# A two-attention kernel whose instruction order is planned by a built-in clock: rounded-part copies issued ahead, transfers modelled in order of arrival

## The chip, the cores and the metric

The kernel runs on one core of one Trainium2 chip. The metric is the device time of one execution in microseconds (us), lower is better. Three runs of the kernel before gave 1972.74, 1975.59 and 1976.52 us; the median is 1975.59 us.

## What is computed

Two attention layers read inputs of their own (x of 2048 x 1024, a joint weight wqkv of 1024 x 3072, an output weight wo of 1024 x 1024, all float32) and their outputs are put side by side. Both have 32 heads of width 32. Layer B is a sliding window of 256 keys. Layer A is a dilated window: 8 keys at distances 0, 2, ..., 14.

```python
def _B_ref(x, wqkv, wo):
    qkv = (x @ wqkv) split into q, k, v of 32 heads x 32
    scores = einsum("bhqd,bhkd->bhqk", q, k) * 32 ** -0.5
    scores = where(0 <= query - key < 256, scores, -1e9)
    return concat_heads(einsum("bhqk,bhkd->bhqd", softmax(scores), v)) @ wo

def _A_ref(x, wqkv, wo):
    # the same with keys at query - 0, 2, 4, ..., 14 (8 of them)
    ...

return concatenate([_A_ref(A_x, ...), _B_ref(B_x, ...)], axis=-1)
```

## The kernel before, in words

**Units and steps.** The 2048 positions of each layer are cut in 4 units of 512 (layer A is first sorted into even and odd positions, so that its window becomes 8 neighbouring keys). Units 0 to 3 are layer B ("dense", a band of 384 keys per 128 queries), units 4 to 7 are layer A ("window", a band of 136). A unit has 8 steps, one for each group of 4 heads: 64 steps in all, numbered hg = 8 * unit + s. All large products are made in three terms: each float32 operand is split into a part rounded to a short format (index 0) and the remainder (index 1), and the product is high x high + high x low + low x high (`TERMS`).

**What a step does.** (1) `qk_items` (L298) multiplies the unit's x by a Q weight and then a K weight: 24 matmuls each, L363. (2) `evac` (L311) brings a result out of PSUM: ScalarE (ACT) writes the rounded part (L314), VectorE (DVE) the remainder (L318) of the tile `nat`. (3) `stack` (L323) has the SyncE queue (SP) issue three SBUF to SBUF copies (L328) that put rounded part and remainder below one another in `qst` (order rounded, rounded, remainder) or `kst` (rounded, remainder, rounded). For units that look back across their border it also reads the last unit's keys (`read_halo`, L304), and writes its own for the next unit. There are two buffers `qst` and two `kst`, used by turns, so the copies of step hg must wait until step hg-2 has read its own. (4) The first pass (`first`, L599): 16 matmuls of scores (L614, called "one" below), each followed by a DVE maximum (L619) and an ACT exponential with a sum (L624). (5) The sums of a step go through a logarithm (L637), a small transpose on PE (`rows`, L653), a copy on DVE (L657) and an SP copy into rows 96 and 97 of `qst` (L660): these are the "row values", the softmax's offset, so that (6) the second pass (L696 dense, L509 window, called "two") gives normalised probabilities straight from an exponential. (7) Masks, then `values` (L741, L548) multiplies by V; `finish` (L570) splits the result for the output product (L577, L581).

**Other streams.** `v_items` makes V in four parts of a unit (L415), `o_items` (L438) multiplies the finished unit by wo (L455), copies the result out of PSUM (`copy_out`, L377: ACT or DVE, whichever the clock believes free earlier) into the one output buffer (`NST = 1`) and stores it from the ACT queue. `Stream` (L87) loads raw weights and x into 3 buffers from the GpSimd queue (POOL), and `parts` (L126) splits each: a cast on DVE, then the subtraction on DVE or POOL.

**What sets the order.** Nothing is scheduled by the compiler. A `Clock` (L33) keeps a believed time for each engine. The main loop (L803) asks the four sequences aux (`rows`), second pass, first pass, gemm (qk, v and o in the order of `plan`) when their next item could start, and puts the earliest on PE; follow-up work is put on its engine when the believed time has come. So a believed duration moves instructions in the program, and on the chip each engine runs its own list strictly in that order, waiting where a semaphore isn't there yet. Believed times of transfers come from `copy`, `load`, `fetch` and `move` (L53 to L76): two believed queues, "copies" (SP) and "loads" (ACT and POOL), that slow each other when both are busy; a copy is believed to start only when the remainder is done. A first pass may be put as soon as `done["stack"]` is believed reached, a second pass when `h["rows"]` is (L661).

**The banks.** Seven PSUM banks are used in rings: 3 for gemm results (`rg`), 4 for scores (`rs`), plus one for the attention output (`ro`).

**The end.** The last unit's output product has no other work to hide behind. The first `TAIL` = 2 output blocks run their first 7 of 8 parts before the last step is finished, and the rest follows (L789 to L797).

Of the kernel before, what the change touches and what calls it, by code (L numbers as in the profile page):

```python
# [25 lines left out]
O_SLOTS = {2: (0, 1), 3: (2, 3), 4: (4, 5), 5: (6, 7)}  # L26
NX, NST = 10, 1
TAIL, LAND, XAT = 2, 0.45, 1
# [4 lines left out]
class Clock:  # L33
# [5 lines left out]
    def __init__(self):  # L39
        self.free = dict(pe=0.0, act=0.0, dve=0.0, pool=0.0, sp=0.0, copies=0.0, loads=0.0)  # L40
        self.later, self.lands = [], []
        self.n = 0
# [9 lines left out]

    def copy(self, dur, *ready):  # L53

        return self.move("copies", "loads", self.use("sp", 0.63, *ready, self.lane()) + 0.4, dur)

    def load(self, dur, *ready):

        return self.move("loads", "copies", self.use("act", 0.35, *ready, self.lane()) + 0.45, dur)

    def fetch(self, dur, *ready):

        t = max(self.use("pool", 1.0, *ready) + 0.6, self.free["loads"])
        self.free["loads"] = t + dur + 0.5 * max(0.0, min(2 * dur, self.free["copies"] - t))
        return self.free["loads"] + LAND
# [21 lines left out]
class Stream:  # L87
# [10 lines left out]
    def load_to(self, n):  # L98
        while self.loaded < min(n, len(self.items)):
# [4 lines left out]
            self.raw[self.loaded] = raw, (self.ck.load if early else self.ck.fetch)(1.9, self.ck.now)  # L104
            self.loaded += 1

    def split_to(self, n):
        while self.split < min(n, len(self.items)):
# [3 lines left out]
            if self.items[i][0] == "x":  # L112
# [10 lines left out]
            end = self.ready[i] if self.items[i][0] != "x" else max(self.ready[i])  # L123
# [23 lines left out]
def kernel(ctx, tc, xs, wqk, wv, wo, outs, units):  # L147
# [23 lines left out]
    for u in range(U):  # L171
        for s in range(NG):
# [3 lines left out]
            if s in V_SLOTS:  # L176
                plan.append(("v", u, V_SLOTS[s]))
# [17 lines left out]
    for p in plan:  # L195
        ly = units[p[1]][0]
        if p[0] == "o":
            item(p, "w", wo[ly, p[2]])
# [99 lines left out]
    def qk_items(u, s):  # L298
# [5 lines left out]
        def read_halo():  # L304
            w = 256 if dense else 128
            hb = halo[(u + 1) % 2][s]
            for r, a in enumerate((0, 1, 0)):
                nc.sync.dma_start(kst[buf][r:96:3, :, 256 - w:256].bitcast(F32), hb[:, a, 256 - w:])
                ck.copy(0.55 if dense else 0.35, ck.now)

        def evac(t, ps, bank):  # L311
# [5 lines left out]
            def low():  # L317
# [556 lines left out]
```

## Time and profile before

| what | value |
|---|---|
| median of 3 runs | 1975.59 us (1972.74 to 1976.52) |
| the profiled execution's own time | 1973.82 us |
| its span, first to last instruction | 1972.1 us |
| granted TensorE clock, mean | 0.987 |
| PE busy | 1924.7 us (98%), 12608 matmuls |
| DVE, ACT, POOL busy | 66%, 49%, 36% |
| DMA, mean over the span | 150 GB/s; SP's queue 26.1% of the engines' time, POOL's loads 22.9% |
| first matmul | at 8.05 us |
| last matmul group (L455) | 1933.17 to 1968.5 us |

The page's chain of work that ended last lies on PE for 84% of the span, on DVE 7%, on DMA 6% and on ACT 2%. A busy PE in this profile includes matmuls that overlap: a matmul of 512 columns shows 401 ns, but the next one starts 227 ns after it when nothing is in the way. So in this text the cost of PE work is the distance from start to start, taken from the trace: 227 ns for 512 columns, 119 ns for 256, 177 ns for a first or second pass of 384, about 85 to 112 ns for one of 136 or 128. Where that distance is longer, PE waited, or ran at half its clock (427 ns).

### The profile page before, as it was taken

To read this page: it belongs to the slowest core of one execution; us is meant where nothing else is said; L and a number is where in the kernel's file an instruction comes from. 1 tells how busy PE (TensorE), PEld (TensorE's weight loads), DVE (VectorE), ACT (ScalarE), POOL (GpSimd) and SP (SyncE) were. 2 spreads that over 40 slices of the span, in tenths; PEclk is the share of its full clock that TensorE was granted. 3 is DMA by queue.
4 is the path that set the end of the run, shared out by engine and by line. 5 is a ranking of instruction groups with operands and counts; after the bars stand their busy time and mean duration, and the time that the engine had idled before them with its cause. 6 is when DMAs were issued, how large, how long until landed. Compare 5 with 4: busy or idle time off the path is not lost.

```text
span 1972.1 us, 36479 instructions
## 1 busy us (share of the span) xinstructions
PE 1924.7 (98%) x12608; PEld 1619.8 (82%) x12608; DVE 1295.7 (66%) x3762; ACT 957.5 (49%) x3137; POOL 708.7 (36%) x923
## 2 busy tenths in 40 slices
PE   7999999999999999999999999999999999999998
PEld 6878887888877878788878888978888788888886
DVE  5687776678665786567865657655666557666653
ACT  3565554475654656555563344423534334434441
POOL 4334343444433434443443323233332333233221
PEclk9999999999999999999999999999989999999998
DMA  5555546455546465345645647455553565556442
GB/s 176 150 139 153 160 124 178 132 153 157 152 136 174 121 189 149 117 140 148 177 119 146 173 139 196 128 149 170 149 163 116 174 177 162 141 146 172 136 126 75
DMA packets 136502, 294.92 MB, mean 150 GB/s; under 512 B 14464, under 2 KB 42112, under 8 KB 136320
## 3 DMA queue, kind: packets, MB, share of 16 engines
q1 hardware_dynamic: 85632, 124.82, 26.1%
q0 software_dynamic: 40320, 146.82, 22.9%
q10 hardware_dynamic: 10368, 20.98, 2.9%
q8 instruction: 100, 1.64, 0.4%
q14 instruction: 82, 0.67, 0.1%
HBM read 163.58 MB, written 27.26 MB: 97 GB/s over the span
## 4 chain that ended last, share of the span: by engine, by line
PE 84%; DVE 7%; DMA 6%; ACT 2%; issue 1%; SPq 0%; POOL 0%; DVEq 0%; ACTq 0%; POOLq 0%
PE g L363 31%; PE g L455 16%; PE g L415 16%; PE s L614 7%; PE s L696 5%; PE o L741 4%; PE s L509 3%; DMA qst<-rt 3%; PE o L548 2%; DMA kst<-nat 1%; DMA raw<-xs 1%; DVE x L137 1%; DVE w L129 1%; ACT s L624 1%; DVE w L137 1%
## 5 line engine op out<-in xcount | busy, mean ns | idle before, releaser
L363 PE MATMUL g<-x,w 128*128 128x512 f32 x3072 | 801.9, 401 | 8.6 <-DVE w L129 8.0
L134 POOL TENSOR_TENSOR w<-raw,w 128x512 fp32r<-128x512 f32 x225 | 392.5, 1745 | 897.2 <-PE s L614 285.7
L363 PEld LDWEIGHTS g<-x,w 128*128 128x128 f32 x3072 | 562.0, 191 | 110.9 <-DVE w L129 8.4
L624 ACT ACTIVATE s<-s,nm 128x384 f32<-128x384 f32 (+3 forms) x1024 | 452.3, 443 | 231.0 <-DVE nm L619 227.1
L415 PE MATMUL g<-w,x 128*128 128x256 f32 x3072 | 413.3, 285 | 0.0
L415 PEld LDWEIGHTS g<-w,x 128*128 128x128 f32 x3072 | 392.7, 191 | 1.9 <-issue 0.6
L455 PE MATMUL g<-ot,w 128*128 128x512 f32 x1536 | 384.2, 397 | 3.6 <-DVE w L129 2.9
L455 PEld LDWEIGHTS g<-ot,w 128*128 128x128 f32 x1536 | 283.8, 190 | 58.1 <-DVE w L129 3.6
L619 DVE CUSTOM_DVE_ANT_0 s<-s,mask_d 128x384 f32<-128x384 f32 (+2 forms) x512 | 262.0, 556 | 72.9 <-PE s L614 71.5
L614 PE MATMUL s<-kst,qst 96*128 96x384 f32 (+3 forms) x1024 | 238.7, 303 | 16.2 <-ACT s L624 7.1
L701 ACT ACTIVATE pbuf<-s 128x384 f32<-128x384 f32 (+2 forms) x480 | 197.1, 507 | 85.5 <-PE s L696 81.8
L614 PEld LDWEIGHTS s<-kst,qst 96*128 96x128 f32 x1024 | 181.3, 192 | 60.5 <-ACT s L624 18.1
L624 ACT ACTIVATION_READ_ACCUMULATOR s<-s,nm 128x1 f32 x1024 | 210.2, 205 | 0.0
L619 DVE CUSTOM_DVE_ANT_0 s<-s,mask_w 128x136 f32<-128x136 f32 (+1 forms) x512 | 142.4, 322 | 98.4 <-PE s L614 96.8
L129 DVE CAST w<-raw 128x1024 fp32r<-128x1024 f32 x256 | 199.9, 781 | 9.4 <-PE g L455 9.4
L137 DVE TENSOR_TENSOR w<-raw,w 128x512 fp32r<-128x512 f32 x287 | 197.2, 696 | 8.8
L682 POOL TENSOR_SCALAR_AFFINE_SELECT pbuf<-pbuf 128x128 f32<-128x128 f32 (+1 forms) x383 | 147.9, 404 | 150.1 <-ACT pbuf L701 143.5
L314 ACT ACTIVATE nat<-g 128x512 fp32r<-128x512 f32 x128 | 76.6, 598 | 255.2 <-PE g L363 247.8
L318 DVE SCALAR_TENSOR_TENSOR nat<-g,nat 128x512 fp32r<-128x512 f32 x128 | 88.3, 690 | 145.5 <-ACT nat L314 134.9
L524 DVE TENSOR_TENSOR pbuf<-pbuf,keep_w 128x272 f32<-128x272 f32 (+1 forms) x224 | 116.9, 566 | 61.5 <-ACT pbuf L514 60.6
L619 DVE DVE_READ_ACCUMULATOR2_ANT nm<- 128x1 f32 x1024 | 144.3, 141 | 0.0
L696 PEld LDWEIGHTS s<-qst,kst 98*128 98x128 f32 x704 | 106.2, 189 | 37.8 <-PE o L741 10.0
(48 smaller groups left out, 1227.3 us busy)
## 6 DMA issues: line engine op xcount, KB each, us to landing
raw<-wqk POOLq DMA_DIRECT2D x126, 512.0 KB, 3.7
qst<-nat SPq DMA_DIRECT2D x192, 256.0 KB
kst<-nat SPq DMA_DIRECT2D x192, 256.0 KB
raw<-wo POOLq DMA_DIRECT2D x64, 512.0 KB, 3.7
raw<-wv POOLq DMA_DIRECT2D x62, 512.0 KB, 4.5
outs<-ost ACTq DMA_DIRECT2D x64, 256.0 KB
raw<-xs POOLq DMA_DIRECT2D x28, 512.0 KB, 4.8
halo<-nat SPq DMA_DIRECT2D x40, 256.0 KB
```

The lines of the kernel that those rows point to most:

```text
L129: nc.vector.tensor_copy(t[:, 0, :], raw)
L134: nc.gpsimd.tensor_tensor(o, a, b, op=ALU.subtract)
L137: nc.vector.tensor_tensor(o, a, b, op=ALU.subtract)
L363: nc.tensor.matmul(h["ps"], h["w"][:, a, k * P:(k + 1) * P], xt[u][k][:, b, :], start=(k == 0 and i == 0), stop=(k == NK - 1 and i == 2))
L415: nc.tensor.matmul(ps, xt[u][k][:, a, p0:p0 + P], h["w"][:, c, k % kw], start=(k == 0 and i == 0 and r == 0), stop=(k == NK - 1 and i == 2 ...
L455: nc.tensor.matmul(h["ps"], h["w"][:, a, k * P:(k + 1) * P], ot[u, k][:, b, :], start=(k == 0 and i == 0), stop=(k == NK - 1 and i == 2))
L614: nc.tensor.matmul(ps[:, :n], q[0:96, j, b * P:(b + 1) * P], kk[0:96, j, c0:c1], start=True, stop=True)
L619: nc.vector.tensor_tensor_reduce(ps[:, :n], ps[:, :n], mask[:, cut:full], scale=-1.0, scalar=BIG, op0=ALU.add, op1=ALU.min, accum_out=nm)
L624: nc.scalar.activation(ps[:, :n], ps[:, :n], AF.Exp, bias=nm, scale=-1.0, accum_out=sm)
L682: nc.gpsimd.affine_select(w, w, pattern=[[0, m], [step, n]], compare_op=ALU.is_ge, fill=0.0, base=base, channel_multiplier=chan)
L696: nc.tensor.matmul(ps[:, i * n:(i + 1) * n], kk[0:98, j, 256 + kb * P:256 + (kb + 1) * P], q[0:98, j, q0:q0 + n], start=True, stop=True)
L701: nc.scalar.activation(w, ps[:, :pack * n].rearrange("p (j n) -> p j n", j=pack), AF.Exp)
```

## The change

It is one change to the planner and to what it plans with; no product, mask or sum is changed.

- *The transfers' model.* The two believed queues become one: every transfer takes its place in the order of arrival (`issue`, `move`), with new lead times, and a raw load of 1.95 us can stand ahead of a copy.
- *Rounded parts ahead.* `stack` is cut in two: `stack_hi` issues the copies of the rounded part when ACT has made it, and `stack` the copy of the remainder when DVE has made that. `read_halo` moves from the K to the Q copies. For K the order becomes rounded, rounded, remainder.
- *Later row values.* `LATE` = 0.4 us is added to the believed landing of the row values, and 30 columns to the believed DVE maximum. The believed landing of the keys, `done["stack"]`, gets no such addition in the diff.
- *V of the first unit* is placed after steps 0, 2, 4, 7 (before: 0, 1, 5, 7).
- *The end.* `TAIL` = 4, the fourth output block takes its bank from the score ring, and the weights of the last five blocks are split as two half tiles each from x's pool ("xw"), so that three weight tiles aren't the limit.

```diff
+V0_SLOTS = {0:0,2:1,4:2,7:3}
...
-TAIL, LAND, XAT = 2, 0.45, 1
+LATE = 0.4
+TAIL, LAND, XAT = 4, 0.45, 1
...
+    def issue(self, eng, hold, lead, dur, *ready):
+        start = max((self.free[eng],) + ready)
+        self.free[eng] = start + hold
+        return self.move(start + lead, dur)
...
     def copy(self, dur, *ready):
-        return self.move("copies", "loads", self.use("sp", 0.63, *ready, self.lane()) + 0.4, dur)
+        self.lands.append(self.issue("sp", 0.63, 1.25, dur, *ready, self.lane()))
+        return self.lands[-1]
...
-    def move(self, q, other, t, dur):
-        t = max(t, self.free[q])
-        self.free[q] = t + dur + 0.5 * max(0.0, min(2 * dur, self.free[other] - t))
-        self.lands.append(self.free[q] + LAND)
-        return self.lands[-1]
+    def move(self, t, dur):
+        busy = self.busy = [x for x in self.busy if x[1] > self.now - 20.0]
+        i = 0
+        while i < len(busy):
+            if busy[i][1] <= t or busy[i][0] < t:
+                t = max(t, busy[i][1])
+            elif busy[i][0] - t >= dur:
+                break
+            else:
+                t = busy[i][1]
+            i += 1
+        busy.insert(i, (t, t + dur))
+        return t + dur + LAND
...
                 def stack():
-                    if t == 1 and has_halo:
-                        read_halo()
-                    dst, c = (qst[buf], 0) if t == 0 else (kst[buf], 256)
-                    for i, a in enumerate((0, 0, 1) if t == 0 else (0, 1, 0)):
-                        nc.sync.dma_start(dst[i:96:3, :, c:c + S].bitcast(F32), hl[:, a, :].bitcast(F32))
-                        e2 = ck.copy(0.95, e, ck.now)
+                    e2 = place(1, e)
                     if t == 1:
-                        done["stack"][u, s] = e2
+                        done["stack"][u, s] = max(e2, h2["hi"])
...
+            def place(part, e):
+                dst, c = (qst[buf], 0) if t == 0 else (kst[buf], 256)
+                for i, a in enumerate((0, 0, 1) if t == 0 else (0, 1, 0)):
+                    if a == part:
+                        nc.sync.dma_start(dst[i:96:3, :, c:c + S].bitcast(F32), hl[:, a, :].bitcast(F32))
+                        e2 = ck.copy(0.95, e, ck.now)
+                return e2
+
+            def stack_hi():
+                if t == 0 and has_halo:
+                    read_halo()
+                h2["hi"] = place(0, r)
...
+        ring = rs if last and n == 3 else rg
...
+            if k == 3 and (not last or n == 0 or n > 2):
+                st.split_to(where["o", u, n] + (3 if last and n == 0 else 2))
+            if k == 5 and last and n in (1, 2):
+                st.split_to(where["o", u, n] + 3)
...
-                e = ck.use("dve", (n + 80) / 960, ck.now)
+                e = ck.use("dve", (n + 110) / 960, ck.now)
...
-                h["rows"] = ck.copy(0.3, e)
+                h["rows"] = ck.copy(0.35, e) + LATE
...
-                one.append(Item(lambda: latest(rs.when(), done["stack"].get((u, s))),
+                one.append(Item(lambda: latest(rs.when(), (done["stack"].get((u, s)))),
```

Building both programs and comparing each engine's list shows that the same 11328 matmuls are issued (a product with V shows as two in the trace), but that almost the whole order on PE, and with it on DVE, ACT, POOL and SP, is different.

More of the change, by code (lines that the diff above doesn't have):

```diff
@@ L39, in __init__ @@
     def __init__(self):
-        self.free = dict(pe=0.0, act=0.0, dve=0.0, pool=0.0, sp=0.0, copies=0.0, loads=0.0)
-        self.later, self.lands = [], []
+        self.free = dict(pe=0.0, act=0.0, dve=0.0, pool=0.0, sp=0.0)
+        self.later, self.lands, self.busy = [], [], []
         self.n = 0
@@ L308, in read_halo @@
                 nc.sync.dma_start(kst[buf][r:96:3, :, 256 - w:256].bitcast(F32), hb[:, a, 256 - w:])
-                ck.copy(0.55 if dense else 0.35, ck.now)
+                ck.copy(0.55 if dense else 0.45, ck.now)
         def evac(t, ps, bank):
@@ L439, in o_items @@
         h = {}
+        last = u == U - 1
+        ring = rs if last and n == 3 else rg
         def ready(k):
@@ L465, in after @@
                 o = stp.tile([P, S], F32, tag="ost", name="ost")
-                e = copy_out(o, h["ps"], h["b"], rg)
+                e = copy_out(o, h["ps"], h["b"], ring)
                 def store():
```

49 lines of the change are left out of this document (27 added, 22 removed).

## The prediction

> **What bounds the kernel now.** I read the page's totals first, then PE's own waits, then the order of time around the longest of them.
>
> ```profile
> span 1972.1 us, 36479 instructions
> PE 1924.7 (98%) x12608; PEld 1619.8 (82%) x12608; DVE 1295.7 (66%) x3762; ACT 957.5 (49%) x3137; POOL 708.7 (36%) x923
> ```
>
> PE has work for nearly the whole span, and the change leaves its work as it is. So the change can only win or lose the time in which PE stands, and what that does to its clock. Who makes PE stand (total us, times, longest):
>
> ```profile
> PE g L363 <- DVE w L129: 8.0, 1, 8.0
> PE s L614 <- ACT s L624: 7.1, 8, 1.2
> PE s L509 <- DMA qst<-rt: 6.7, 10, 1.8
> PE s L614 <- DMA kst<-nat: 5.7, 5, 2.0
> PE s L653 <- DVE hl L645: 3.4, 10, 0.5
> PE g L455 <- DVE w L129: 2.9, 1, 2.9
> PE s L696 <- DMA qst<-rt: 2.4, 4, 0.8
> ```
>
> The first is the start. Row values (qst<-rt) cost 9.1 us and keys (kst<-nat) 5.7 us: these are what the change is about. Start to start, which also shows what overlapping matmuls hide, PE loses some 76 us to single delays over 0.15 us.
>
> How keys get to `kst`, at step 49, in the order of time (start, length, what, idle before it):
>
> ```profile
> 1495.93 0.60 ACT L314 ACTIVATE nat<-g 128x512 fp32r<-128x512 f32 x1 [5.00 <-PE g L363]
> 1496.56 1.93 SPq L328 DMA_DIRECT2D kst<-nat  x3
> 1496.56 0.69 DVE L318 SCALAR_TENSOR_TENSOR nat<-g,nat 128x512 fp32r<-128x512 f32 x1 [3.39 <-ACT nat L314]
> 1502.88 0.63 PE L614 MATMUL s<-kst,qst 96*128 96x128 f32 x4 [0.90 <-DMA kst<-nat]
> ```
>
> The first copy leaves at 1496.56, when ACT is done and DVE has just begun: on the chip the rounded part is already copied ahead. Only the clock didn't know.
>
> A late row value, steps 46 and 47:
>
> ```profile
> 1446.55 0.91 PE L363 MATMUL g<-x,w 128*128 128x512 f32 x3
> ...
> 1448.75 0.69 SPq L660 DMA_DIRECT2D qst<-rt  x1
> ...
> 1450.65 0.69 PE L614 MATMUL s<-kst,qst 96*128 96x136 f32 x2 [0.97 <-ACT s L624]
> ...
> 1453.14 0.58 PE L509 MATMUL s<-qst,kst 98*128 98x8 f32 x4 [1.80 <-DMA qst<-rt]
> 1453.58 1.55 PE L363 MATMUL g<-x,w 128*128 128x512 f32 x3
> ```
>
> After two idle stretches of 0.97 and 1.80 us the same three matmuls take 1.55 us instead of 0.91: the clock has fallen.
>
> The end, on PE and DVE, and the busy time of PE, PEld, DVE, ACT, POOL with the granted clock there:
>
> ```profile
> 1931.83 0.69 DVE L382 COPY ost<-g 128x512 f32<-128x512 f32 x1 [4.06 <-DMA outs<-ost]
> 1932.43 0.69 DVE L129 CAST w<-raw 128x1024 fp32r<-128x1024 f32 x1
> ...
> 1933.17 35.35 PE L455 MATMUL g<-ot,w 128*128 128x512 f32 x144 [2.85 <-DVE w L129]
> 1905.00:1940.00 35.00, 30.08 (x195) 23.58 (x194) 18.58 (x53) 11.75 (x41) 5.95 (x7) 0.76 0.21 71
> ```
>
> An output copy on DVE waits for the store before it (one buffer), and the weight cast behind it makes PE wait.
>
> **The change part by part.** I lay the changed program's PE order beside the old one, price the PE work between a producer and its consumer by start-to-start distances (227 ns for 512 columns, 119 for 256, 177 for a pass of 384), and compare it with the time the chip needed in the trace.
>
> *Row values, -12 us.* From `rows` on PE to the landing plus 0.13 us takes 2.9 to 5.0 us, mean 3.7 (52 steps where the copy wasn't held up). The old order has less than 4.2 us of work in that gap in 37 steps of 64, the new one in 15. That removes what undelayed steps lose outside the last one, some 6 us of the 9.1. At steps 38, 46, 54 the DVE copy (L657) stands behind maxima and x splits, and 6.6 to 7.6 us are needed: the gap grows from 4.5, 3.2, 4.5 to 5.3, 5.4, 5.3 us, +0.8, +2.2, +0.8, about 3.5 us. The half clock after such pairs costs 10 matmuls x 0.2 us at 1454 to 1464 and some 5 at each of the other two; I count 2.5 saved. Bounds: -3 (only the undelayed half) and -18.
>
> *The logarithm, -1 us.* `rows` itself (L653 behind L645) loses 8.6 us from start to start in 19 steps. The work between the last first pass and `rows` grows in nine of these (steps 18 and 29 by 2 and 3.4 us) and shrinks in eight (step 6 from 8.9 to 2.2). Where it grows 3.6 us can go, where it shrinks as much can come: bounds -4 and +3, and I take -1.
>
> *Step 0, -2 us.* Keys were needed after 7.1 us of work, now after 9.3; the stall was 2.17 us. Only where the start slips is it less: 0 to -2.2.
>
> *The end, -6 us.* From the last `rows` (1917.51) to the last matmul's start (1968.14) are 50.6 us, and its work is 38.4: 12.2 are lost, in waits of 1.4 (L509), 0.7 and 2.85 us and at the half clock (the 0.76 above). With four blocks begun, 18 + 3 + 12 output matmuls and then 21 (4.8 us) stand where PE stood, so the first three waits go. But now blocks 1, 2 and 3 are copied out by DVE in a row, each waiting for the store before it: 2.16 us from the end of a copy to the next (1929.67 to 1931.83), plus 0.69. Block 0 ends 5.5 us after the last value matmul; its copy ends at 6.3, the others at 9.2, 12.2, 15.1. The split for block 5 stands behind them on DVE; PE comes to it at 13.0 and stands until the cast is done, 15.6: 2.6 us, 0.5 more for the remainder, and 2 to 3 us of half clock, as after the old wait of 2.85. 12 - 6 = 6; bounds 0 and -12 (no such wait).
> [...] I keep -6.
>
> *Keys, +11 us.* This is the edit that speaks against the change. Issuing the rounded parts first moves SP's last K issue from 2.4 to 2.3 us after the projection's last matmul starts, for the first already left before the remainder: a real gain of 0.1 us. The believed landing after that matmul's end falls from 6.1 us (remainder done at 1.6, three issues, transfers, LAND) to 5.4 (rounded part at 0.8). The trace needs 6.2 us at best and 7.2 on average (39 steps with a free SP; raw loads make the difference). LATE isn't added here. So the first pass comes earlier than keys do: in 19 steps (18, 26, 33, 34, 37 to 39, 42, 45 to 47, 50, 53 to 55, 58, 61 to 63) the work in the gap is 5.85 us on average, 7.2 before. Steps of a similar kind needed 6.8, now 6.7: 19 x 0.85 = 16 us, against some 5 of theirs now. Bounds: 5 - 4 = +1 (every landing at its best) and 19 x (7.1 - 5.85) - 4 = +20.
>
> *Keys behind step hg-2, +5 us.* Where SP waits for step hg-2's second pass, the trace has 9.4 us (no halo) or 12.6 (three more copies) from its last matmul to the landing. Step 7 now has 25.0 us of work where 20.1 + 9.4 are needed: 4 us. Steps 14, 22, 30 have 16.2 where 5.3 + 12.6 are: 1.3 each. Of these 8 us I take 3 off, for stalls at 207 to 218 us (4 us before L614 and L653) that this order partly dissolves. Bounds 0 and +11 (with half clock).
>
> *The rest, 0, -8 to +8.* `read_halo` moves ahead of three Q issues on SP; the page has SP waiting most of the time, and Q has 5.5 us before K. The maximum's believed cost becomes 0.515 us, which is what rows show from start to start (0.51). But ACT still runs evacuations and output copies ahead of waiting exponentials (L624 behind L314 at 469.08), and the new order has as many such places. V's new slots move work in unit 0 alone.
>
> Sum: -12 - 1 - 2 - 6 + 11 + 5 = -5. Against the profiled execution's own 1973.8 us that is 1968.8; the median of the runs lies 1.8 us above that execution, so 1970.6.
>
> **The rivals.** (A) *Rounded copies do land sooner*, as the clock believes: if transfers, not SP, set the landing and start 0.7 us sooner, the keys' +11 becomes 0 and step hg-2's +5 becomes +3: -12 - 1 - 2 - 6 + 3 = -18, 1957.6. Against it stands the issue row at 1496.56. (B) *Slower: keys become the limit everywhere.* The 19 steps meet raw loads as the worst half did (+20), step hg-2's cost is +8, pairs of short stalls halve the clock as at 1453 (+7 for five such places), and the row values then save only 6: -6 - 1 - 2 - 6 + 20 + 8 + 7 = +20, 1995.6. It decides when the two key terms pass 21 together, the sum of all that is saved. For it: landings of 7.4 to 9.8 us in a third of the steps. Against: most clean landings are in window units, where the tight steps are. (C) *No change*: each removed wait shows again at the next one (ring of four score banks, L614 behind L624), 1975. For it: 98% busy, and the exponentials' places are unchanged. Against: the end is outside of this, and gives its part anyway.
>
> **How the numbers follow.** Forecast 0.38, A 0.24, B 0.26, C 0.12. A measurement of this kernel can tell about 0.2% (4 us) from no change, so the forecast's own range, 1964 to 1976, lies on both sides of 1971.6: 0.26 of it faster, 0.12 same. Faster: 0.26 + 0.24 = 0.50; same: 0.12 + 0.12 = 0.24; slower: 0.26. For 8 in 10 the range reaches beyond A's 1957.6, for the row values' bound, and half way into B: 1950 to 1990.
>
> **What would show it.** Right: qst<-rt as a releaser of PE falls from 9.1 us to under 4; kst<-nat rises from 5.7 to 15 or more, with idle times of 0.3 to 1.5 us before L614 in the steps named and about 4 us at step 7; SP's first K copy still starts as ACT's evacuation ends; in the last 40 us one wait of 2 to 3 us on a DVE cast of x<-raw behind a copy of ost. Wrong: kst<-nat under 8 us (A), or over 25 us with a granted clock below 0.98 (B); a wait of ACT's exponentials grown by as much as the row values saved (C).

## The result, and the profile after

The changed kernel takes 1981.91 us in the median of 8 runs (1978.73 to 1993.33), the kernel before 1972.94 us on the same chip (8 runs). The ratio is 1.0055 with a 95% interval of 1.0040 to 1.0071: slower by about 11 us, where 5 us faster was forecast. The profiled execution took 1985.16 us. Its totals and the waits of PE (total us, times, longest):

```profile
span 1983.5 us, 36517 instructions
PE 1931.2 (97%) x12608; PEld 1619.3 (82%) x12608; DVE 1288.1 (65%) x3748; ACT 956.3 (48%) x3136; POOL 718.9 (36%) x943
```

```profile
PE s L651 <- DMA kst<-nat: 8.6, 11, 1.5
PE g L392 <- DVE w L144: 8.1, 2, 7.9
PE s L651 <- ACT s L661: 6.7, 6, 1.2
PE s L651 <- DVE rt L694: 4.1, 3, 2.0
PE s L651 <- DMA kst<-halo: 4.0, 5, 1.5
PE s L651 <- issue: 3.5, 4, 2.5
PE s L733 <- ACT pbuf L738: 2.8, 2, 2.0
PE s L690 <- DVE hl L682: 2.7, 3, 2.1
PE g L490 <- DVE x L144: 2.1, 1, 2.1
...
PE s L733 <- DMA qst<-rt: 0.7, 1, 0.7
```

Lines have moved: L614 of before is L651, L363 is L392, L696 is L733, L509 is L546, L653 is L690, L455 is L490. Row values (qst<-rt) stood at 9.1 us and are at 0.7. Keys stood at 5.7 and are at 12.6 with the five waits that the profile puts down to `kst<-halo`. Those behind "issue" (3.5) and the one of a first pass behind L738 (0.8) are keys too: in the trace each of these first passes, and each of the five, starts 0.09 to 0.46 us behind the landing of its own step's keys. So keys cost 16.9 us of idle time (5.9 before, counted in the same way). First passes behind DVE (L694) grew from 1.6 us to 4.1, and second passes behind ACT's exponentials (L738) are new. So one wait was taken away, another one grew, and some came up that the prediction had not named.

These waits are only what shows as idle. The table below sums, for each item on PE, its distance from the start of the item before it, less what that earlier item costs when nothing is in the way (the distances given with the profile before). What stands behind the last `rows` is counted apart. The values' base is somewhat too high, so there only differences count. A row goes by the item's place, not by who released it. All are from one execution of each kernel, which isn't the median one: it took 0.9 us more than the median before (1972.94 us), and against the median of its own runs 3.3 us more after, 2.3 less in e3, 1.8 more in e5, 6.2 less in e13, 7.5 more in e4 and 0.3 more in e7. The run labels are explained below.

| us lost on PE | before | after | e3 | e5 | e13 | e4 | e7 |
|---|---|---|---|---|---|---|---|
| first of the first passes (keys) | 8.4 | 20.8 | 11.7 | 34.7 | 13.5 | 5.9 | 4.6 |
| first of the second passes (row values) | 12.9 | 3.4 | 3.1 | 7.0 | 3.6 | 3.4 | 3.5 |
| `rows` (logarithm) | 8.5 | 3.7 | 12.3 | 4.4 | 9.2 | 6.2 | 5.7 |
| other first passes | 26.1 | 28.7 | 28.3 | 28.5 | 24.0 | 23.0 | 20.6 |
| other second passes | 17.9 | 23.3 | 14.3 | 19.5 | 14.1 | 25.2 | 15.2 |
| values | -8.6 | -3.3 | -7.9 | -2.5 | -8.7 | -5.0 | -4.9 |
| products at half clock | 18.7 | 25.6 | 14.9 | 22.7 | 14.8 | 23.8 | 21.1 |
| other products | 37.5 | 38.1 | 37.8 | 40.4 | 37.1 | 37.8 | 37.8 |
| behind the last `rows` | 12.2 | 4.8 | 3.7 | 3.2 | 4.7 | 4.8 | 4.5 |
| sum | 133.5 | 145.1 | 118.2 | 158.1 | 112.3 | 125.1 | 108.3 |

Step 61 shows how keys come late now, in the order of time:

```profile
1861.26 0.60 ACT L330 ACTIVATE nat<-g 128x512 fp32r<-128x512 f32 x1 [0.91 <-PE g L392]
1861.88 1.98 SPq L354 DMA_DIRECT2D kst<-nat  x3
1861.89 0.69 DVE L334 SCALAR_TENSOR_TENSOR nat<-g,nat 128x512 fp32r<-128x512 f32 x1 [0.20 <-ACT nat L330]
...
1868.19 0.64 PE L651 MATMUL s<-kst,qst 96*128 96x136 f32 x4 [1.50 <-DMA kst<-nat]
```

SP issues three copies in 1.98 us from 0.02 us behind ACT's end, as it did in 1.93 us at step 49 before: the chip does with the cut `stack` what it did without it. Only the first pass stands earlier, and PE waits 1.50 us. Twelve steps lose over 0.5 us in this way (26, in a dense unit, and 37, 42, 45 to 47, 50, 53, 58, 61 to 63 in window units), 14.0 us together, all twelve among the 19 that the prediction named.

Steps 46 and 47, where a row value had come late:

```profile
1463.98 0.44 PE L651 MATMUL s<-kst,qst 96*128 96x136 f32 x2 [0.92 <-DVE rt L694]
...
1469.04 0.69 PE L651 MATMUL s<-kst,qst 96*128 96x136 f32 x2 [0.98 <-ACT s L661]
1469.76 0.89 PE L546 MATMUL s<-qst,kst 98*128 98x8 f32 x6
```

The second pass (L546) no longer waits, but the first passes ahead of it do, one for a bank that DVE reads (L694), one for an exponential.

The end, on DVE and PE, and then the busy time of PE, PEld, DVE, ACT, POOL with the granted clock there:

```profile
1957.46 0.69 DVE L411 COPY ost<-g 128x512 f32<-128x512 f32 x1 [2.17 <-DMA outs<-ost]
...
1960.32 0.69 DVE L411 COPY ost<-s 128x512 f32<-128x512 f32 x1 [2.17 <-DMA outs<-ost]
1960.93 0.42 DVE L144 CAST x<-raw 128x512 fp32r<-128x512 f32 x1
...
1961.40 18.51 PE L490 MATMUL g<-ot,x 128*128 128x512 f32 x72 [2.12 <-DVE x L144]
```

```profile
1905.00:1951.00 46.00, 44.08 (x340) 38.31 (x339) 28.61 (x91) 18.00 (x73) 11.06 (x13) 1.00 0.34 101
```

Copies wait 2.17 us each for the store before them, the cast of block 5 stands behind them, and PE waits 2.12 us once.

The largest surprise lies at the ends of the dense units. The same view for three stretches (in brackets the number of instructions, for PE of matmuls; behind POOL the granted clock), first before, then after, then after without the cut of `stack` (e13, below):

```profile
400.00:460.00 60.00, 60.00 (x433) 51.55 (x432) 46.65 (x129) 37.75 (x111) 26.91 (x42) 1.00 0.57 156
670.00:740.00 70.00, 68.39 (x446) 56.34 (x445) 56.73 (x158) 42.38 (x124) 29.24 (x46) 1.00 0.55 157
940.00:1010.00 70.00, 68.38 (x467) 57.10 (x460) 55.76 (x149) 41.75 (x122) 29.12 (x48) 0.98 0.52 148
```

```profile
400.00:460.00 60.00, 58.48 (x391) 47.20 (x390) 42.77 (x114) 35.05 (x102) 25.39 (x42) 0.97 0.53 144
670.00:740.00 70.00, 66.74 (x409) 52.57 (x408) 50.98 (x134) 40.37 (x117) 26.97 (x45) 0.95 0.56 155
940.00:1010.00 70.00, 66.25 (x397) 52.11 (x396) 50.54 (x132) 38.09 (x110) 27.03 (x45) 0.93 0.50 140
```

```profile
400.00:460.00 60.00, 58.66 (x409) 49.05 (x408) 45.90 (x121) 36.66 (x106) 26.09 (x43) 1.00 0.53 147
670.00:740.00 70.00, 66.79 (x434) 54.63 (x434) 55.11 (x145) 42.57 (x122) 30.72 (x51) 1.00 0.53 155
940.00:1010.00 70.00, 66.66 (x461) 54.38 (x461) 55.41 (x147) 41.53 (x120) 30.97 (x53) 1.00 0.49 143
```

After the change the clock falls to 0.97, 0.95 and 0.93 there, and fewer matmuls stand in the same time (their sizes differ between the programs, so the count alone is no rate). What PE does at the first of the three, and below it a row of the kernel before:

```profile
428.96 2.76 PE L733 MATMUL s<-qst,kst 98*128 98x128 f32 x12
431.65 2.47 PE L778 MATMUL o<-pbuf,vbuf 128*32 128x128 f32 x24
434.05 0.98 PE L733 MATMUL s<-qst,kst 98*128 98x384 f32 x4
...
437.52 0.91 PE L392 MATMUL g<-x,w 128*128 128x512 f32 x3
439.73 1.18 PE L651 MATMUL s<-kst,qst 96*128 96x384 f32 x3 [1.29 <-DMA kst<-nat]
440.71 1.48 PE L392 MATMUL g<-x,w 128*128 128x512 f32 x3
```

```profile
439.05 1.50 PE L741 MATMUL o<-pbuf,vbuf 128*32 128x128 f32 x24
```

Twelve second passes and 24 value products stand in a row with no projection (L392) between them. The last four of these second passes each start 0.05 us behind the end of an exponential (L738), and value products at 432.11, 432.87 and 433.25 start 0.02 to 0.03 us behind that of a mask on POOL (L719). So PE waits here for ACT and for the masks that follow it, and 24 value products take 2.47 us, which took 1.50 us at 439.05 in the kernel before. Then comes a key wait of 1.29 us (step 14, whose copies waited for step 12's second pass), and three projections take 1.48 us in place of 0.91. The trace's clock record stands at full until 439.86 us and at half for the 3.4 us behind it, so what is lost before that is waiting and not a slower clock.

Not every fall of the clock there belongs to the change. Between 400 and 1030 us the record has one piece at half before (3.4 us at 989.45) and six after (at 439.86, 470.57, 706.10, 736.82, 972.33 and 1006.47, 23.9 us together). Those at 470.57, 736.82 and 1006.47 come with a 1.25 us wait of a first pass for an exponential that the kernel before has as well, at 470.29, 730.5 and 988.4; its clock fell at the last of them alone. The first of them, before and then after:

```profile
470.29 2.13 PE L614 MATMUL s<-kst,qst 96*128 96x384 f32 x4 [1.25 <-ACT s L624]
472.26 1.55 PE L363 MATMUL g<-x,w 128*128 128x512 f32 x6
```

```profile
468.96 2.37 PE L651 MATMUL s<-kst,qst 96*128 96x384 f32 x4 [1.25 <-ACT s L661]
471.13 2.76 PE L392 MATMUL g<-x,w 128*128 128x512 f32 x6
```

Behind the same wait six projections take 1.55 us in one execution and 2.76 in the other. Over the whole execution the record has 52.7 us at half before and 50.4 after: this time moved, from the window units and the end to the ends of the dense units.

### The profile page after: what moved, and what is told of

The parts are those of the page before. It is cut to its first block, busy times and chain, and to the rows that moved or that the text cites. A ratio compares the mean times of both kernels' runs of the same rounds, so it can differ in the third digit from the quotient of the medians.

```text
span 1983.5 us, 36517 instructions
## 1 busy us (share of the span) xinstructions
PE 1931.2 (97%) x12608; PEld 1619.3 (82%) x12608; DVE 1288.1 (65%) x3748; ACT 956.3 (48%) x3136; POOL 718.9 (36%) x943
## 4 chain that ended last, share of the span: by engine, by line
PE 87%; DMA 5%; DVE 4%; ACT 2%; issue 1%; SPq 1%; DVEq 0%; ACTq 0%
PE g L392 34%; PE g L490 16%; PE g L444 16%; PE s L651 7%; PE s L733 4%; PE o L778 4%; PE s L546 3%; DMA kst<-nat 2%; PE o L585 2%; DVE w L144 1%; ACT s L661 1%; DMA qst<-nat 1%; DMA kst<-halo 1%; DVE pbuf L722 1%; DVE x L152 1%
## 5 line engine op out<-in xcount | busy, mean ns | idle before, releaser
L392 PE MATMUL g<-x,w 128*128 128x512 f32 x3072 | 805.9, 402 | 8.7 <-DVE w L144 8.1
L149 POOL TENSOR_TENSOR w<-raw,w 128x512 fp32r<-128x512 f32 x231 | 402.9, 1744 | 887.0 <-issue 330.8
L392 PEld LDWEIGHTS g<-x,w 128*128 128x128 f32 x3072 | 562.9, 192 | 113.9 <-DVE w L144 8.9
L490 PE MATMUL g<-ot,w 128*128 128x512 f32 x1416 | 360.0, 397 | 1.3 <-DVE ot L618 1.3
L490 PEld LDWEIGHTS g<-ot,w 128*128 128x128 f32 x1416 | 259.2, 190 | 48.5 <-DVE ot L618 1.7
L651 PE MATMUL s<-kst,qst 96*128 96x384 f32 (+3 forms) x1024 | 238.5, 305 | 28.8 <-DMA kst<-nat 8.6
L651 PEld LDWEIGHTS s<-kst,qst 96*128 96x128 f32 x1024 | 179.3, 192 | 75.5 <-issue 24.4
L738 ACT ACTIVATE pbuf<-s 128x384 f32<-128x384 f32 (+2 forms) x480 | 199.1, 507 | 64.7 <-PE s L733 48.3
L719 POOL TENSOR_SCALAR_AFFINE_SELECT pbuf<-pbuf 128x128 f32<-128x128 f32 (+1 forms) x397 | 148.0, 391 | 164.4 <-ACT pbuf L738 158.4
L144 DVE CAST w<-raw 128x1024 fp32r<-128x1024 f32 x251 | 195.9, 780 | 0.1
L152 DVE TENSOR_TENSOR w<-raw,w 128x512 fp32r<-128x512 f32 x271 | 185.8, 692 | 8.6
L561 DVE TENSOR_TENSOR pbuf<-pbuf,keep_w 128x272 f32<-128x272 f32 (+1 forms) x224 | 107.2, 524 | 59.4 <-ACT pbuf L551 58.1
L733 PEld LDWEIGHTS s<-qst,kst 98*128 98x128 f32 x704 | 108.8, 189 | 43.4 <-ACT s L661 12.9
```

The lines of the kernel that those rows point to most:

```text
L144: nc.vector.tensor_copy(t[:, 0, :], raw)
L149: nc.gpsimd.tensor_tensor(o, a, b, op=ALU.subtract)
L152: nc.vector.tensor_tensor(o, a, b, op=ALU.subtract)
L392: nc.tensor.matmul(h["ps"], h["w"][:, a, k * P:(k + 1) * P], xt[u][k][:, b, :], start=(k == 0 and i == 0), stop=(k == NK - 1 and i == 2))
L490: nc.tensor.matmul(h["ps"], w[:, a, c:c + P], ot[u, k][:, b, :], start=(k == 0 and i == 0), stop=(k == NK - 1 and i == 2))
L651: nc.tensor.matmul(ps[:, :n], q[0:96, j, b * P:(b + 1) * P], kk[0:96, j, c0:c1], start=True, stop=True)
```

## The experiments

Each was timed beside the kernel before on one chip (medians of before: 1969.33 us for e1 to e4, 1967.36 for e5 to e8, 1970.73 for e9 to e12, 1968.71 for e13 to e16), so the ratios are what is compared; 0.001 is 2 us. The ratio isn't the quotient of the two medians, which lies up to 0.0018 away from it; a difference of 0.002 between two runs of the table is hardly more than noise.

| run | what | median us | ratio, 95% |
|---|---|---|---|
| e1 | before, K's rounded copies first | 1971.49 | 1.0002 (0.9987 to 1.0016) |
| e2 | before, the end alone | 1963.43 | 0.9969 (0.9954 to 0.9983) |
| e3 | e2, row values 0.45 later | 1960.78 | 0.9947 (0.9929 to 0.9966) |
| e4 | after, keys 0.8 later | 1957.78 | 0.9925 (0.9901 to 0.9948) |
| e5 | e3, `stack` cut | 1997.20 | 1.0148 (1.0128 to 1.0168) |
| e6 | e3, one queue | 1964.65 | 0.9989 (0.9975 to 1.0002) |
| e7 | e4, maximum n + 80 | 1948.35 | 0.9898 (0.9879 to 0.9916) |
| e8 | after, keys 0.4 later | 1962.61 | 0.9983 (0.9967 to 0.9999) |
| e9 | after, maximum n + 80 | 1978.94 | 1.0024 (1.0004 to 1.0045) |
| e10 | e3, maximum n + 110 | 1964.52 | 0.9972 (0.9953 to 0.9990) |
| e11 | e7 with 1.4 for 0.8 | 1962.70 | 0.9944 (0.9919 to 0.9969) |
| e12 | after, V's slots as before | 1983.95 | 1.0053 (1.0032 to 1.0074) |
| e13 | after, `stack` uncut | 1958.82 | 0.9957 (0.9938 to 0.9976) |
| e14 | e3, keys 0.8 later | 1952.25 | 0.9926 (0.9907 to 0.9945) |
| e15 | after, keys 1.0 later | 1955.40 | 0.9937 (0.9915 to 0.9958) |
| e16 | e15, maximum n + 80 | 1950.46 | 0.9917 (0.9898 to 0.9936) |

**e1: the copies' order alone**, on the kernel before; the clock is told nothing.

```diff
-                    for i, a in enumerate((0, 0, 1) if t == 0 else (0, 1, 0)):
+                    for i, a in ((0, 0), (1, 0), (2, 1)) if t == 0 else ((0, 0), (2, 0), (1, 1)):
```

> The kernel before with one thing changed: SP issues the K copies as rounded, rounded, remainder (before: rounded, remainder, rounded). The clock is told nothing, so every engine's order stays as it was. Theory (the rounded copies already left early): SP's last K issue moves by 0.1 us, the first passes' waits on keys stay at 8.4 us within 2, the time within 0.1% of before (1971 to 1975). Rival (rounded copies ahead really bring keys 0.7 us sooner): the waits on keys fall under 4 us and the time by 4 us or more.

1.0002. On the chip the order of the three copies is worth nothing that can be seen, and the rows at 1496.56 and 1861.88 have the first copy leave as ACT ends (0.03 and 0.02 us behind it) without and with the cut. So what the cut does, it does through the clock's belief; the move of `read_halo`, which belongs to it, was not tried alone. Rival A is refuted.

**e2: the end alone** (`TAIL` = 4, the fourth block in the score ring, half tiles), on the kernel before. Here, and in e3, e5, e6, e10 and e14, that block also waits for the last step's values, which it doesn't in the change.

```diff
-TAIL, LAND, XAT = 2, 0.45, 1
+TAIL, LAND, XAT = 4, 0.45, 1
...
+        ring = rs if last and n == 3 else rg
```

> The kernel before with the change's end alone: TAIL 4, the fourth block on the score ring (and only after the last step's values), half tiles for the last five weights. Theory: the order up to the last steps is that of before; after the last rows 12.2 us of loss become about 5, with one wait of 2 to 3 us on a cast behind output copies; the time falls by 7 us, to about 1966. Rival (the end gives its gain back, since copies and stores queue up): loss after the last rows stays over 10 us, time within 2 us of before.

0.9969, 6 us of gain where 7 were forecast. The loss behind the last `rows` went from 12.2 to 6.0 us.

**e3: the end, and row values later** in the old clock.

```diff
-                h["rows"] = ck.copy(0.3, e)
+                h["rows"] = ck.copy(0.3, e) + 0.45
```

> As the one with the end alone, and row values believed to land 0.45 us later, in the clock of before (two queues, keys as before). Theory (row values cost 9 us and can be hidden by this alone): second passes' first waits fall from 12.9 to about 5 us, keys rise by some 3 to 5 us as the order moves, time about 1961 to 1964. Rival (a wait taken from the row values comes back in other waits of the attention items): first waits fall, but the other waits rise by as much, time as with the end alone.

0.9947. The first of the second passes fell from 10.5 (e2) to 3.1 us, and `rows` rose from 8.6 to 12.3: a net of 3.7 us, and 0.0022 of the time (4 us), with intervals that overlap.

**e4 and e8: the keys later too**, in the changed kernel: 0.8 us, and LATE's own 0.4 us.

```diff
-                        done["stack"][u, s] = max(e2, h2["hi"])
+                        done["stack"][u, s] = max(e2, h2["hi"]) + 0.8
```

> The changed kernel with keys believed to land 0.8 us later (added to done[stack]), nothing else. Theory (keys believed too early are what made it slower): first passes' waits on keys fall from 20.8 to about 10 us and the time by 8 to 11 us, to 1971 to 1974. Rival (the order in which attention items stand without products beside them is what made it slower): waits on keys fall by about 10 us, but the other waits stay or grow, and the time stays over 1978.

> The changed kernel with LATE's 0.4 us on the keys too, as it has for the row values. Theory: key waits fall with the dose: the order leaves 24.1 us of landings uncovered against 35.0 (changed kernel) and 17.2 (0.8 us, where 5.9 us were measured), so keys cost 10 to 13 us in place of 20.8, and the rest stays as it is in both: 1966 to 1972 us. Rival: it is not the dose but a luckier order that made 0.8 us fast: no relation, anything from 1955 to 1985 us, with keys at 8 us or less or at 18 or more.

0.9925 and 0.9983 against 1.0055: 26 and 14 us come back, and the key waits go from 20.8 to 5.9 and 13.7 us. The dose decides the sign of the whole change. e4's forecast, 8 to 11 us, was missed: more came back than its key waits. e8 was faster than forecast, for second passes (19.0 us) and half clock (20.7) came down with the keys.

**e5 and e6: one part each on top of e3**, the cut of `stack`, or the one-queue Clock.

```diff
-                    for i, a in enumerate((0, 0, 1) if t == 0 else (0, 1, 0)):
...
+                    e2 = place(1, e)
...
+            def stack_hi():
+                if t == 0 and has_halo:
+                    read_halo()
+                h2["hi"] = place(0, r)
```

> The run with the end and the later row values (0.9947 of the time before, 1960.8 us) plus one edit: `stack` is cut in two as in the change, so the clock believes the K copies of the rounded part issued as ACT ends and takes the keys to land earlier. Theory: the belief alone brings first passes ahead of their keys. In this program's order the work between a K projection and its first pass leaves 48.5 us of the landings of the trace uncovered, against 19.9 us without the edit; the keys measured 0.6 of such an estimate so far (11.7 us there), so they cost about 28 us, +16 to +18, and the time is 1974 to 1980 us. Rival: the cut is a matter of the copies' order, which alone changed nothing (1.0002), and the key wait came from the one-queue model: 1959 to 1963 us.

> The run with the end and the later row values plus the change's Clock alone (one queue in order of arrival, its lead times), with the copies issued as before. Theory: the queue model does little; uncovered key landings by the order are 18.1 us against 19.9, row values 4.8 against 4.9, so 1958 to 1962 us. Rival: the one-queue model, which lets a raw load stand ahead of a copy and moves every believed landing, is what cost the 13 to 20 us outside of keys, row values and end: 1972 us or more, with cold products (18 us or less in the kernel before) at 24 us.

The waits of e5 (its first pass is L637):

```profile
PE s L637 <- DMA kst<-nat: 15.3, 12, 4.3
PE s L637 <- issue: 10.4, 10, 2.3
```

The ten waits behind "issue" are keys here too: each of these first passes starts 0.09 to 0.31 us behind the landing of its keys. The cut cost 40 us there (1.0148 against 0.9947), more than twice the forecast: 23 us as key waits, 8 as half clock, 5 each in other second passes and values. e6 lies between its two forecasts: 0.0042 slower than e3 (8 us), of which its profile shows 4.3 as key waits; it isn't nothing, and it isn't the 13 to 20 us of the rival.

**e7 and e9: the believed maximum as before**, with keys 0.8 later and without.

```diff
-                e = ck.use("dve", (n + 110) / 960, ck.now)
+                e = ck.use("dve", (n + 80) / 960, ck.now)
```

> The changed kernel with 0.8 us more on the believed landing of the keys (1957.8 us) and the believed DVE maximum back at n + 80 columns (30 columns, 31 ns, less). Theory: the dearer maximum stretches the believed attention past the projections at the unit ends, and what is left there runs alone, one item per exponential, with PE at half its clock. By the order, stretches of attention items alone beyond 2 us add up to 6.5 us with this edit and 17.4 without; cold products should fall from 23.8 to 15 to 18 us and other second passes from 25.2 to 17 to 20, together 10 to 16 less: 1943 to 1950 us. Rival: what stands at the unit ends is due to the other beliefs (the row values' LATE, V's slots) or any order loses so much: cold and second passes stay, 1955 to 1960 us.

> The changed kernel, its keys without any addition, with only the believed DVE maximum back at n + 80. Theory: the two causes are separate and add up. Keys stay near 18 to 21 us (the order leaves 30.5 us of landings uncovered, 35.0 in the changed kernel), other second passes fall from 23.3 to about 15: 8 to 12 less than the changed kernel, 1968 to 1975 us, so about the time of the kernel before. Rival: the maximum mattered only together with the later keys: 1978 to 1985 us.

e7 is the fastest of all, 0.9898. Other second passes fell from 25.2 to 15.2 us, further than forecast; half clock only from 23.8 to 21.1. e9 gave 0.0031 (6 us) where 8 to 12 were forecast, and its time, 1978.94 us, falls at the fast edge of the rival's. But other second passes went down from 23.3 to 17.2 us, and the gain is no smaller than with the later keys (0.0027, e7 against e4): nothing shows that the maximum needs them. The three stretches in e7:

```profile
400.00:460.00 60.00, 59.06 (x411) 49.30 (x409) 45.17 (x114) 34.64 (x98) 30.75 (x50) 1.00 0.52 147
670.00:740.00 70.00, 68.48 (x463) 55.51 (x462) 53.55 (x136) 42.24 (x120) 35.45 (x60) 1.00 0.53 161
940.00:1010.00 70.00, 68.49 (x465) 57.28 (x464) 55.01 (x145) 39.68 (x115) 28.84 (x48) 0.98 0.53 154
```

The clock is back at 1.00, 1.00 and 0.98, as in the kernel before. In the profiled executions read here the low clock goes with n + 110 and not with the cut. With n + 80 none has less in these stretches than e1, which has the order of before (1.00, 0.98, 0.98): e3, e9 and e5, which has the cut, have 1.00 in all three, e16 has 1.00, 1.00 and 0.98. With n + 110, e4 has 0.97, 0.98 and 1.00, e15 0.97, 0.98 and 0.98, e8 and e12 the 1.00, 0.98 and 0.98 of e1, and e10, with neither the cut nor the one queue, has 0.97, 1.00 and 0.95 (its rows stand below). e13, n + 110 without the cut, is the exception with 1.00 in all three. So, as far as one execution of each can say, the loss of clock at the unit ends doesn't need the cut, and n + 110 doesn't bring it in every order.

**e10: the dearer maximum on e3**, where by the order it leaves no more of such stretches than without it.

> The run with the end and the later row values (1960.8 us) plus the believed maximum at n + 110. Theory: the 31 ns cost nothing by themselves; they only do so where they leave attention items alone at the unit ends, and by the order they don't here (9.3 us of such stretches against 10.4): other second passes stay at 14 to 16 us and the time at 1957 to 1964 us. Rival: a dearer maximum always draws the believed attention out: second passes 20 us or more, 1967 us or more.

0.9972 against 0.9947, 5 us above e3, with intervals that overlap: between the two forecasts. Second passes stayed (16.0 us), as the theory had it. The extra time of the profiled execution lay in keys (21.6 us against 11.7), and its clock fell at the unit ends all the same:

```profile
400.00:460.00 60.00, 56.75 (x381) 46.55 (x380) 41.51 (x121) 38.90 (x116) 24.52 (x40) 0.97 0.53 138
940.00:1010.00 70.00, 66.57 (x417) 53.94 (x416) 52.26 (x139) 40.50 (x117) 27.34 (x46) 0.95 0.52 147
```

```profile
449.66 0.59 PE L624 MATMUL s<-kst,qst 96*128 96x384 f32 x2 [3.15 <-DMA kst<-nat]
...
451.83 1.49 PE L363 MATMUL g<-x,w 128*128 128x512 f32 x3
```

Step 14 waits 3.15 us for its keys there, without the cut. So the theory's reason, that the 31 ns cost nothing where the order leaves no attention items alone, failed in this execution. It is the slowest of twelve (1975.44 us), and why its keys came late was not explained.

**e11: still later keys**, 1.4 us.

> The fastest version so far (keys 0.8 us later, maximum at n + 80, 1948.4 us) with 1.4 us for the keys. Theory: by the order uncovered key landings fall from 16.2 to 6.0 us, of which 4.6 us were left as measured waits, and uncovered row values rise from 4.7 to 6.9: -3 and +2, 1944 to 1951 us, the dose has run out. Rival: later first passes gain still (cold products at 21 us are due to keys): cold falls to 16 or less, 1940 us or less.

Both forecasts missed: 0.9944, slower than with 0.8. Its waits, and below them those of e7:

```profile
PE s L690 <- DVE hl L682: 5.0, 8, 2.2
PE s L651 <- ACT s L661: 5.0, 8, 0.9
PE s L546 <- DMA qst<-rt: 4.4, 3, 2.2
```

```profile
PE s L690 <- DVE hl L682: 2.5, 2, 2.0
...
PE s L546 <- DMA qst<-rt: 1.6, 2, 0.9
```

In this one execution of each, later first passes push the logarithm and the row values against their consumers: `rows` waits 2.5 us more, row values 2.8 more, and other second passes rose from 15.2 to 21.8 us.

**e12: V's slots of the first unit as before.**

```diff
-V0_SLOTS = {0:0,2:1,4:2,7:3}
+V0_SLOTS = V_SLOTS
```

> The changed kernel with V of the first unit after steps 0, 1, 5, 7 again. Theory: the slots are worth a little and not the loss; the order leaves 38.9 us of keys uncovered (35.0) and 21.0 us of attention items alone (18.0), row values 5.9 (1.7): +4 to +9, 1985 to 1992 us. Rival: the new slots brought the attention of the dense units out of step with the projections: without them second passes and cold products fall, 1970 us or less.

1.0053 against 1.0055: the slots did nothing that can be seen, neither the small gain nor the loss.

**e13 to e16: the cut undone alone, the key delay without it, and a further pair for the maximum.** e13 has `stack` as before and all else as changed; e14 is e3 with 0.8 us on `done["stack"]`; e15 and e16 differ in the maximum.

> The changed kernel with `stack` as before (three copies together, when the remainder is done; keys' halo with K), everything else as changed. Theory: the cut is the part that makes it slower, through the belief that keys land when the rounded part's copies and the remainder's do. Uncovered key landings by the order are 20.3 us in place of 35.0 and attention items alone 9.2 us in place of 18.0: key waits 11 to 16 us, other second passes 15 to 18, time 1963 to 1971 us, faster than before. Rival: the cut only helps the one-queue clock to be right, and the loss comes from the new queue and the maximum: 1978 us or more.

> The run with the end and the later row values (1960.8 us, 11.7 us of key waits) with 0.8 us more on the keys too: no cut, no new queue, old maximum. Theory: a microsecond of key waits costs more than itself (25 us came back for 15 us of waits in the changed kernel), so 6 to 8 us less of them (the order leaves 7.3 us uncovered, 19.9 without) gives 8 to 13 us: 1948 to 1953 us. Rival: outside of the cut the keys' waits cost only what they last and later first passes push row values: 1955 to 1961 us.

> The changed kernel with 1.0 us on the keys, believed maximum n + 110; pair of the next run. Theory: the dearer maximum costs 4 to 7 us as in three pairs so far (0.25 to 0.31%), here through attention items alone (17.6 us of such stretches by the order): 1954 to 1959 us and 0.2 to 0.4% above the next. Rival: nothing, the two agree within 0.1%.

> The same with the believed maximum at n + 80. Theory: between the 0.8 us version (1948.4 us) and the 1.4 us version (1962.7 us, where row values and second passes came to wait): uncovered keys 13.4, row values 3.6, attention alone 6.2 us by the order, all a little less than at 0.8 us: 1945 to 1952 us. Rival: the dose had run out before 1.0: 1955 us or more.

e13 is 0.9957: without the cut the change is faster than before by 8 us, with it slower by 11. The cut alone costs 0.0098 (19 us), and undoing it turns the sign, as later keys do. e14's median lies in the range forecast, but by the ratio it is 0.0021 (4 us) faster than e3, against 8 to 13 forecast, with intervals that overlap; its key waits fell by 2.8 us. That a key wait costs more than it lasts in any order is not shown. e15 stands 0.0020 above e16, as forecast, and both medians lie in their ranges. The four pairs for the maximum give 0.0020 to 0.0031 each: 4 to 6 us. No pair is clear of noise alone, since the two intervals of each overlap; that all four point the same way is the evidence.

## Why the prediction was wrong

Its steps, one by one, by the table and the runs:

- *Row values, -12*: right as a wait. The first of the second passes went from 12.9 to 3.4 us in the changed kernel; their idle is 0.7 us (under 4 was asked). But alone (e3 against e2) they brought 4 us, because `rows` took half of it back there.
- *The logarithm, -1*: mis-sized. `rows` went from 8.5 to 3.7 us after the change; it has 12.3 in e3 and 9.2 in e13, so it follows the order and is not a gain of this edit.
- *Step 0, -2*: the stall went from 2.17 to 1.39 us, -0.8.
- *The end, -6*: right, alone (e2, 6 us) and in the changed kernel (12.2 to 4.8 us), by the wait that was named: 2.12 us behind the output copies. The half clock behind it is there too: 1.00 is granted in the 46 us shown, and 0.94 over 1951 to 1983, which is 2 us.
- *Keys, +11, and those behind step hg-2, +5*: right as waits. Keys lost 12.4 us more, where -2 + 11 + 5 = 14 were added up, and the late steps were those named. Steps 14, 22 and 30 lost 1.46, 0.96 and 0.20 us for 1.3 each. At step 7 hardly any of the 4 us came: the copies landed 9.4 us after step 5's second pass, as forecast, but 30.4 us lay between the projection and the first pass for 25.0 us of work, since PE had already lost time to other waits (2.14 us before `rows` at 206.76, and the 3.4 us at half clock from 207.75 on). As an idle time keys rose to 16.9 us, where 15 or more was the sign asked for; the releaser's name shows only part of it.
- *The rest, 0 (-8 to +8)*: this is the step that failed. In the profiled execution other first passes lost 2.6 us more, other second passes 5.4, values 5.3 and products at half clock 6.9: +20. The prediction held that the dearer maximum was the truer number, and that the new order had as many places of waiting exponentials as the old. The first was half right: from the start of a maximum of 384 columns to the start of DVE's next operation, the trace of before has 0.47 to 0.49 us in 167 cases, as n + 80 has it (0.483), and 0.51 to 0.52 in 163, as n + 110 has it. The second was a count of places; it left out the stretches in which attention stands with no projection between. Of the +20, the runs put 4 to 6 us on the maximum. Without the cut (e13) the four items together are at 44.2 us, 10 less than before and 30 less than after, so in this order it is with the cut that they come. These two executions are 32.6 us apart where the ratios say 19, largely because one lies above its median and the other below; up to 18.6 of the 32.6 us are the clock's, by an estimate: half of the difference between 50.4 and 13.3 us at half clock, where the output product's matmuls (L490 after) stand 427 ns apart, and 227 at full clock. So the cut's price of 19 us is only in part the keys' (20.8 against 13.5 us in e13), and the 26 us of e4 are more than its 15 us of key waits.

Summed up, the waits that were forecast came nearly as forecast (row values, logarithm and end -21.7 for -19, keys with step 0 +12.4 for +14), and the loss arose beside them, in a term that stood at 0. Rival B had the right sign with the wrong mechanism: neither key term reached its price, and the clock of the whole (0.988, 0.987 before) did not fall. The half clock, which it added, did come at the unit ends (23.9 us between 400 and 1030 us, 3.4 before), in place of half clock elsewhere. Rival C's condition, a wait of ACT's exponentials grown by what the row values saved, is in part what happened (L733 behind L738, 2.8 us, and longer distances that show no idle). The record goes to half 0.13 us behind the end of a wait of 1.29 us after the change (at 439.86), and 0.52 us behind the end of one of 1.80 us, with 0.97 us shortly ahead of it, before (at 1453.66); the waits of 1.25 us at 470.29 and 730.5 before had no such fall behind them. What makes the clock fall was not shown.

What stays open: how the cut and the 31 ns of the maximum lead through the planner to the losses at the unit ends. In the changed program they shrink when either is taken back (e13, e9), but e10 has the fall of the clock there without the cut, and e9 as much half clock over the whole execution (47.3 us) as after. The longer believed times of halo copies, loads and stores (0.35 to 0.45, 1.9 to 1.95, 0.8 to 0.85 us), which e13 has and e6 hasn't, were not tried alone. Parts do not add up either: the end and row values (-10 us in e3), the one queue (+8) and the maximum (+5) would make e13 slower than before by 3 us, and it was faster by 8.

The fastest version, e7, is the change with the keys 0.8 us later than the clock computes and the maximum as before: 1948.35 us, 0.9898 (0.9879 to 0.9916) of the time before. Its interval overlaps those of e16 (1.0 us) and of e14, which has neither the cut nor the one queue; so it isn't shown that these two parts gain anything even with later keys.

## What to carry to other kernels

A planner's model of transfers must be made later on every path that it speeds up: this change corrected the row values and, by cutting `stack`, moved the keys the other way, and 0.4 us on 64 believed landings decided the sign (1.0055 against 0.9983). Copies that already leave early on the chip gain nothing by being believed earlier (without that belief e13 was 19 us faster), and a delay can be too long: 0.8 us paid (0.9898, e7), and 1.4 us pushed the wait to the next consumer (0.9944, e11). When an order is new almost everywhere, forecast not only the waits that the edit touches but the stretches in which one kind of work stands alone: in the case shown PE went at the pace of ACT's exponentials and of the masks (2.47 us for 24 value products, 1.50 before), and its clock fell to half for 3.4 us behind the wait of 1.29 us that followed.

## What the runs showed of the hardware

The clock records of the profiled executions of before and after hold only full and half. Before, seven pieces at half end ahead of the last instruction: three of 3.4 us, two of 6.8, one of 10.2 and one of 17.1; after, eleven: eight of 3.4 us and three of 6.8. With one more at the end of each record (1.6 and 2.8 us) they are 52.7 us together before and 50.4 after; the same sum is 20.2 in e3, 54.3 in e5, 13.3 in e13 and 20.5 in e7.

The granted clock of one and the same program varied between executions: for the kernel before, 24 runs on one chip (those beside e9 to e12) had 0.984 to 0.993 and 1983.2 to 1965.3 us, about 1.7 us for each 0.001. Runs of a few microseconds' difference can't be told apart by one profile, and the row "products at half clock" of the table carries this spread.

The gain of e3 came with a granted clock of 0.995 in the median of its runs, against 0.988 for the kernel before: at 1.7 us for 0.001 that is, by an estimate, as much as its whole gain of 10 us. How much of the gain came as shorter waits and how much as clock was not separated.
